# Two heads' blocks of 64 queries in one tile of 128 partitions, and 64 attention steps for 80

## The chip, the cores and the metric

The kernel runs on one core of a Trainium2 chip. The core's engines have a queue of instructions each and meet at semaphores: TensorE (PE in the profile; PEld is its loading of stationary operands), VectorE (DVE), ScalarE (ACT), GpSimd (POOL) and SyncE (SP), which here issues the DMAs. The metric is the device time of one execution in microseconds (us).

## What is computed

Causal attention over B=4 batches, H=8 heads, S=576 tokens and D=64, blended per head with a read of a linear memory, and behind it two gated MLPs over all 2304 tokens. In short:

```
a      = softmax(q k^T / 8, causal);  local = a v
q_p    = phi(q)                       # phi(x) = max(x, 0) + exp(min(x, 0))
mem    = (q_p M_prev) / (q_p . z_prev + 1e-6)
x      = g mem + (1 - g) local        # g = sigmoid(beta) of the head; heads side by side: 2304 x 512
x      = (sigmoid(x w_gate) * (x w_val)) w_out        # 512 -> 1536 -> 512
h      = x w_in;  out = (h * clip(h + 3, 0, 6) / 6) w_out2    # 512 -> 2048 -> 512
```

## The kernel before

The program has three phases. Phase A does the attention and, laid between its pieces, the gate and value products of the first MLP (the first half of its hidden features, six of twelve groups of 128, for the first 1872 tokens, in six chunks of 312). Phase B does the rest of the first MLP, phase C the second MLP.

Two heads are handled together, one in partitions 0 to 63 of the transposed queries and keys, the other in 64 to 127. The 576 query rows of a head are cut into blocks (`QB`): block 0 has 64 rows, blocks 1 to 4 have 128. Blocks 0, 1, 2 are the first range, 3 and 4 the second. A visit is one pair of heads and one range; there are 32 visits, and in each batch the four pairs' first ranges come before the four second ranges (`VISITS`). A block of a visit is a step: three steps in a visit of the first range, two in one of the second, 80 in all. A step does for its block and both heads:

- scores (`score_part`, L259): one matmul a head with 128 stationary query columns, into a PSUM tile of a pool of four which the MoE's products also use. For block 0 the stationary operand holds rows 64 to 127 too, which are not used later;
- one pass of DVE over each score tile, which adds the causal mask, scales and takes the row's extreme (L263), and one exponential a head on ACT with the row's sum (L280).

After the range's last step DVE makes the reciprocals of the sums with the gate's factor (L303, L304), and the rows are normalized (`normalize`), on ACT in steps 6 to 33 and for block 4, else on DVE (L309, L311). In the same rows, left of the attention weights, stand 64 columns of phi(q) over its norm (`prep_phi`, `memory_rows`; DVE, ACT and GpSimd), so that the memory read and the weighted sum of v are one product. Three steps later PE transposes the rows (`transpose_bank`, L322), up to four 128x128 pieces to a PSUM bank, ACT copies each bank to SBUF (L325), and the value products follow (`pv`, L348). Their result is stored to DRAM as `xd`, and a chunk of the MoE reads it back (`moe_x`, `xc<-xd`), splits it in a rounded part and a rest (L164, L165) and uses it two steps later at the earliest.

The order of PE's queue is that of the code in `phase_a`. A step is: scores, the transposes of two banks, a value product, then, if more is due, half of the step's share of MoE units, the rest of the scores and one more bank, then the other half of the share. A unit is three matmuls of 312 columns (L169 to L171). The share depends on the chunk (`FILL`). Where the next chunk is not there yet, no MoE unit is laid down. The order on DVE, ACT, GpSimd and SP is made by a scheduler. The first MLP's weights are loaded as pairs of 32-bit words and converted by DVE and ACT (`convert`, L134 to L143), one group every third step from step 6 on, nine groups.

Of the kernel before, what the change touches and what calls it, by code (L numbers as in the profile page):

```python
# [34 lines left out]

_T = [
    [(g, i, j) for g in range(2) for i, j in ((0, 0), (1, 0), (2, 0), (1, 1), (2, 1), (2, 2))],
    [(g, i, j) for g in range(2) for j in range(5) for i in (3, 4) if j <= i],
]
BANKS = [  # L40
    [_T[0][0:4], _T[0][4:8], _T[0][8:12]],
    [_T[1][4 * n : 4 * n + 4] for n in range(5)],
]
# [6 lines left out]
FILL = (4, 9, 6, 9, 6, 6)  # L50
# [10 lines left out]
PW = [384, 640]  # L61
# [4 lines left out]
class Kernel:  # L66
# [9 lines left out]
    def setup(self):  # L76
# [6 lines left out]
        self.bt_sb = cp.tile([128, H], F32, name="bt_sb")  # L83
# [4 lines left out]
    def attn_consts(self, pool):  # L88
# [14 lines left out]
        self.a1 = pool.tile([128, H], F32, name="a1")  # L103
        self.a2 = pool.tile([128, H], F32, name="a2")
# [77 lines left out]
    def load_visit(self, v):  # L182
# [6 lines left out]
        a = self.pa2.tile([128, 20 * D], F32, name="aux", tag="aux", bufs=3)  # L189
        qn = a[:, 0 : 10 * D].rearrange("p (e j d) -> p e j d", e=2, j=5)  # L190
        (t0, n), j0, j1 = RTOK[ranges[0]], RANGES[ranges[0]][0], RANGES[ranges[0]][-1] + 1
# [3 lines left out]
        if h == 0 and 0 in ranges:  # L195
            z = self.pa2.tile([128, H, D], F32, name="zz", tag="zz", bufs=1)
            nc.sync.dma_start(z, self.zz[b : b + 1].rearrange("o h d -> o (h d)").broadcast_to([128, H * D]))
            self.z = z
        nc.sync.dma_start(
            qn[:, :, j0:j1, :],  # L200
            src[:, 0 : 10 * D].rearrange("p (e j d) -> p e j d", e=2, j=5)[:, :, j0:j1, :],
        )
        v1 = 10 * D + j1 * 2 * D
        nc.sync.dma_start(a[:, 10 * D : v1], src[:, 10 * D : v1])
# [5 lines left out]
            "qn": qn,  # L210
            "v": a[:, 10 * D :].rearrange("p (j c) -> p j c", j=5),
        }

    def prep_phi(self, v):
# [5 lines left out]
        h0 = vs["pair"][1]  # L220
        blocks = [i for rg in vs["ranges"] for i in RANGES[rg]]
        nb = len(blocks)
        js = slice(blocks[0], blocks[-1] + 1)
        ph = self.pa2.tile([128, 2, nb, D], F32, name="ph", tag="ph")
        w = self.pa1.tile([128, 2, nb, D], F32, name="phw", tag="phw")
# [191 lines left out]
    def phase_a(self):  # L417
# [47 lines left out]
        while t < nt or tq or vq:  # L465
# [10 lines left out]
            if t < nt and i == RANGES[rg][1]:  # L476
                self.memory_rows(v, rg)
# [19 lines left out]
            if t >= 6 and t % 3 == 0:  # L497
                self.w_convert()
# [225 lines left out]
```

## Time and profile before

| | |
|---|---|
| median of 3 runs | 1108.28 us (1107.02 to 1108.61) |
| the profiled execution's own time | 1105.09 us |
| its span | 1103.3 us |
| PE busy | 1068.7 us, 97% |
| DVE busy | 625.0 us, 57% |
| ACT busy | 521.9 us, 47% |
| POOL busy | 58.5 us, 5% |
| mean granted PE clock | 0.991 of full speed |

The profiled execution is one run under the profiler; its span goes from the first to the last instruction that the profile shows, 1.8 us less than its time. PE's busy time counts a pipelined matmul until its modelled end, so 97% does not say that PE is at its peak. The shares are means over the whole span: phases B and C, from about 412 us on, are nearly PE alone, while DVE's and ACT's load lies in phase A. A granted clock of 1.00 is 2.4 GHz, 0.50 is 1.2 GHz.

### The profile page before, as it was taken

How to read it: one execution, taken by the hardware profiler on the slowest of the kernel's cores; microseconds unless marked ns; L12 is line 12 of the kernel's file. 1: busy time of each engine (PE TensorE's matmuls, PEld its weight loads, DVE VectorE, ACT ScalarE, POOL GpSimd, SP SyncE). 2: the span in 40 equal slices, each digit the busy share in tenths (PEclk: the TensorE clock that was granted, in tenths of full speed). 3: DMA queues.
4: the chain of work that ended last, by engine and by line, in shares of the span. 5: the costliest groups of instructions: out<-in, count | busy, mean ns of one | idle time of the engine just before them, and what ended most of it. 6: DMA issues, size and time to landing. Idle time of an engine off the chain costs nothing.

```text
span 1103.3 us, 16108 instructions
## 1 busy us (share of the span) xinstructions
PE 1068.7 (97%) x5984; PEld 921.0 (83%) x5984; DVE 625.0 (57%) x1526; ACT 521.9 (47%) x1161; POOL 58.5 (5%) x72
## 2 busy tenths in 40 slices
PE   6689999999999999999999999999999999999998
PEld 4357768887888789999888888999998999999897
DVE  7999975464546428988898348933232232322322
ACT  6899885557555645344443134433233232232322
POOL 2212111100110000000000000000000000000000
PEclk9889999999999999999999999999999999999999
DMA  6565532333233305334353224301001010010000
GB/s 218 165 212 164 192 111 84 109 89 102 83 102 94 91 15 206 115 108 163 131 188 112 70 89 154 110 1 58 1 1 58 1 58 1 21 37 1 29 1 29
DMA packets 58223, 98.54 MB, mean 89 GB/s; under 512 B 5665, under 2 KB 42529, under 8 KB 58145
## 3 DMA queue, kind: packets, MB, share of 16 engines
q1 hardware_dynamic: 58144, 97.51, 27.1%
q8 instruction: 47, 0.77, 0.3%
q14 instruction: 32, 0.25, 0.1%
HBM read 79.50 MB, written 17.99 MB: 88 GB/s over the span
## 4 chain that ended last, share of the span: by engine, by line
PE 84%; DVE 6%; DMA 4%; ACT 3%; issue 1%; SPq 0%; POOL 0%; ACTq 0%; DVEq 0%
PE g L171 12%; PE g L170 12%; PE g L169 11%; PE acc L647 6%; PE acc L648 6%; PE acc L649 6%; PE m L169 5%; PE m L171 4%; PE m L170 4%; PE pv L348 4%; PE t L322 3%; PE s L259 3%; PE acc L171 3%; PE acc L169 3%; PE acc L170 3%; DMA xc<-xd 2%
## 5 line engine op out<-in xcount | busy, mean ns | idle before, releaser
L170 PE MATMUL g<-xs,wslot 128*128 128x384 f32 (+2 forms) x672 | 235.3, 351 | 0.0
L171 PE MATMUL g<-xs,wslot 128*128 128x384 f32 (+2 forms) x672 | 235.3, 351 | 0.0
L169 PE MATMUL g<-xs,wslot 128*128 128x384 f32 (+2 forms) x672 | 230.7, 351 | 0.0
L636 DVE SCALAR_TENSOR_TENSOR th<-th,g 128x384 f32<-128x384 f32 x96 | 53.2, 554 | 219.8 <-ACT th L635 219.5
L635 ACT ACTIVATE th<-g,three 128x384 f32<-128x384 f32 x96 | 55.8, 581 | 219.6 <-PE g L171 218.7
L170 PEld LDWEIGHTS g<-xs,wslot 128*128 128x128 f32 x672 | 126.1, 188 | 9.2
L169 PEld LDWEIGHTS g<-xs,wslot 128*128 128x128 f32 x672 | 126.0, 188 | 8.7
L171 PEld LDWEIGHTS g<-xs,wslot 128*128 128x128 f32 x672 | 126.1, 188 | 6.8
L647 PE MATMUL acc<-wslot,hs 128*128 128x512 f32 x288 | 113.7, 395 | 0.0
L648 PE MATMUL acc<-wslot,hs 128*128 128x512 f32 x288 | 113.5, 394 | 0.0
L164 ACT CAST hs<-th 128x384 fp32r<-128x384 f32 (+2 forms) x132 | 69.9, 529 | 87.0 <-DVE th L636 49.6
L649 PE MATMUL acc<-wslot,hs 128*128 128x512 f32 x288 | 109.0, 393 | 0.0
L280 ACT ACTIVATE P<-P,m 128x64 f32<-128x64 f32 (+4 forms) x160 | 89.4, 561 | 35.2 <-DVE m L263 32.7
L165 DVE TENSOR_TENSOR hs<-th,hs 128x384 fp32r<-128x384 f32 (+2 forms) x132 | 76.1, 577 | 49.9 <-ACT hs L164 49.3
L169 PE MATMUL m<-xs,wslot 128*128 128x312 f32 x288 | 94.3, 327 | 0.0
L322 PEld LDWEIGHTS t<-ident,P 128*128 128x128 f32 x480 | 57.0, 147 | 38.6 <-issue 24.5
L322 PE MATMUL t<-ident,P 128*128 128x128 f32 x480 | 73.8, 291 | 15.3 <-issue 10.1
L170 PE MATMUL m<-xs,wslot 128*128 128x312 f32 x288 | 88.2, 306 | 0.0
L171 PE MATMUL m<-xs,wslot 128*128 128x312 f32 x288 | 87.9, 305 | 0.0
L259 PE MATMUL s<-qk 64*128 64x320 f32 (+4 forms) x384 | 78.8, 468 | 8.2 <-DMA qk<-in_qk 5.9
L263 DVE CUSTOM_DVE_ANT_0 P<-s,mask 128x320 f32<-128x320 f32 (+3 forms) x160 | 65.6, 429 | 17.3 <-PE s L259 16.8
L325 ACT COPY T<-t 128x512 f32<-128x512 f32 (+2 forms) x128 | 66.1, 541 | 9.8 <-PE t L322 9.7
(74 smaller groups left out, 1768.7 us busy)
## 6 DMA issues: line engine op xcount, KB each, us to landing
wst<-in_wm SPq DMA_DIRECT2D x68, 512.0 KB, 4.4
aux<-in_aux SPq DMA_DIRECT2D x32, 192.0 KB, 2.6
qk<-in_qk SPq DMA_DIRECT2D x32, 160.0 KB, 2.5
aux<-in_aux SPq DMA_DIRECT2D x16, 320.0 KB, 3.3
qk<-in_qk SPq DMA_DIRECT2D x16, 288.0 KB, 3.2
x<-x SPq DMA_DIRECT2D x6, 768.0 KB, 4.5
out<-xp SPq DMA_DIRECT2D x18, 256.0 KB, 2.0
xc<-xd SPq DMA_DIRECT2D x24, 156.0 KB, 2.2
```

The costliest lines, as they stand in the source:

```text
L164: (ehi.copy if ehi is self.nc.scalar else ehi.tensor_copy)(hi, src)
L165: elo.tensor_tensor(lo, src, hi.bitcast(F32), op=ALU.subtract)
L169: nc.tensor.matmul(out, w[0], x[0], start=first, stop=False)
L170: nc.tensor.matmul(out, w[0], x[1], start=False, stop=False)
L171: nc.tensor.matmul(out, w[1], x[0], start=False, stop=last)
L259: nc.tensor.matmul(ps[:, : e - a], qk[rows, 0, q0 : q0 + 128], qk[rows, 1, a:e], start=True, stop=True)
L280: self.nc.scalar.activation(x, x, AF.Exp, bias=vs["m", rg][:, g, n : n + 1], scale=-1.0, accum_out=vs["l", rg][:, g, n : n + 1],)
L322: nc.tensor.transpose(ps[:, c : c + 128], src, self.ident)
L325: nc.scalar.copy(pr["T", rg][:, o : o + c], ps[:, :c])
L647: nc.tensor.matmul(a, gs[:, 0, cc], w[:, 0, :], start=(f == 0), stop=False)
L648: nc.tensor.matmul(a, gs[:, 0, cc], w[:, 1, :], start=False, stop=False)
L649: nc.tensor.matmul(a, gs[:, 1, cc], w[:, 0, :], start=False, stop=(f == FF2 - 1))
```

## The change

Block 0 of the two heads, 64 query rows each, now shares one tile of 128 partitions: head 0's rows in partitions 0 to 63, head 1's in 64 to 127. A range's rows are a list of tiles (`ROWS`): in the first range the shared one and blocks 1 and 2 of both heads, five tiles for six; in the second range four, as before. The shared tile has no step of its own. Its scores are two matmuls with 64 stationary columns and 64 moving ones, written into columns 192 to 255 of the PSUM tile that holds the second head's scores of block 1 (L299 of the changed kernel), and a third DVE pass with a mask of its own (`mask0`) and a third exponential belong to that step. So a first range has two steps, `UNITS` (0, 1) and (2), and the attention 64 steps. What follows is changed to fit: per-row gate factors and z_prev come laid out by tile from the host, z_prev in three DMAs; phi is computed for five tiles; the first range has 11 transposes for 12; in the value products' output head 1 has its blocks in order and head 0 has block 0 behind blocks 1 and 2, so that the store is three DMAs. The numbers counted in steps are set anew: MoE units a step (`FILL`), the steps in which ACT normalizes, and the weight conversion, every second step from step 5 on.

```diff
+ROWS = [[None] + [(g, i) for g in range(2) for i in (1, 2)], [(g, i) for g in range(2) for i in (3, 4)]]
 _T = [
-    [(g, i, j) for g in range(2) for i, j in ((0, 0), (1, 0), (2, 0), (1, 1), (2, 1), (2, 2))],
+    [(1, 0), (2, 0), (0, 0), (3, 0), (4, 0), (1, 1), (2, 1), (3, 1), (4, 1), (2, 2), (4, 2)],
...
+UNITS = [[(0, 1), (2,)], [(3,), (4,)]]
...
-FILL = (4, 9, 6, 9, 6, 6)
+FILL = (5, 9, 8, 9, 8, 8)
...
+        self.mask0 = pool.tile([128, 64], F32, name="mask0")
+        for g in range(2):
+            rows = slice(64 * g, 64 * g + 64)
+            nc.gpsimd.tensor_copy(self.mask0[rows], self.mask[rows, 448 + 64 * g : 512 + 64 * g])
...
+            nc.sync.dma_start(flat(z[:, 0:H]), one(self.zz[b : b + 1, 0:H]).broadcast_to([128, H * D]))
+            for g in range(2):
+                h0 = H + H // 2 * g
+                nc.sync.dma_start(
+                    flat(z[64 * g : 64 * g + 64, H:]),
+                    one(self.zz[b : b + 1, h0 : h0 + H // 2]).broadcast_to([64, H // 2 * D]),
+                )
...
+        if rg == 0:
+            nc.gpsimd.tensor_tensor(w[:, 0], ph[:, 0], vs["z"][:, H + h0 // 2], op=ALU.mult)
+        r0 = nb - 4
+        z = vs["z"][:, h0 : h0 + 2, :].unsqueeze(2).to_broadcast([128, 2, 2, D])
+        heads = lambda a: a[:, r0:].rearrange("p (g n) d -> p g n d", g=2)
+        nc.gpsimd.tensor_tensor(heads(w), heads(ph), z, op=ALU.mult)
...
+    def row_max(self, v, rg, r, ps, a, e, mask):
+        m = self.visits[v]["m", rg][:, r : r + 1]
+        self.nc.vector.tensor_tensor_reduce(
+            out=self.row(v, rg, r, 64 + a, 64 + e),
+            in0=ps,
+            in1=mask,
...
             nc.tensor.matmul(ps[:, : e - a], qk[rows, 0, q0 : q0 + 128], qk[rows, 1, a:e], start=True, stop=True)
             tiles.append(ps)
+        if i == 1:
+            for g in range(2):
+                rows = slice(64 * g, 64 * g + 64)
+                nc.tensor.matmul(
+                    tiles[1][rows, e : e + 64], qk[rows, 0, 0:64], qk[rows, 1, 0:64], start=True, stop=True, skip_group_check=True
+                )
         for g, ps in enumerate(tiles):
+            self.row_max(v, rg, ROWS[rg].index((g, i)), ps[:, : e - a], a, e, self.mask[:, off + a : off + e])
+        if i == 1:
+            self.row_max(v, rg, 0, tiles[1][:, e : e + 64], 0, 64, self.mask0)
...
-        for g in range(2):
-            x = vs["P", rg][:, g, n, 64 : 128 + 128 * i]
+        for r in [ROWS[rg].index((g, i)) for g in range(2)] + [0] * (i == 1):
+            x = self.row(v, rg, r, 64, row_at(rg, r)[1])
...
             if rg == 0:
-                T = pr["T", rg][:, 704 * g : 704 * g + 704]
-                mine = [(0, 0, T[:, 0:320]), (1, 64, T[:, 320:576]), (2, 192, T[:, 576:704])]
+
+                o = 64 * g
+                mine = [(0, 0, 320 * g, 320), (1, o, 640 + 256 * g, 256), (2, o + 128, 1152 + 128 * g, 128)]
...
-        nc.sync.dma_start(self.xd[h // 2, :, b * S + t0 : b * S + t0 + nt], x[:, :nt])
+        dst = self.xd[h // 2, :, b * S + t0 : b * S + t0 + nt]
+        if rg == 0:
+            nc.sync.dma_start(dst[64:], x[64:, :nt])
+            nc.sync.dma_start(dst[:64, 64:], x[:64, : nt - 64])
+            nc.sync.dma_start(dst[:64, :64], x[:64, nt - 64 : nt])
+        else:
+            nc.sync.dma_start(dst, x[:, :nt])
...
-        steps = [(v, rg, i) for v, (p, ranges) in enumerate(VISITS) for rg in ranges for i in RANGES[rg]]
+        steps = [(v, rg, u[-1]) for v, (p, ranges) in enumerate(VISITS) for rg in ranges for u in UNITS[rg]]
...
-                    self.normalize(v, rg, 6 <= t < 34)
+                    self.normalize(v, rg, 5 <= t < 27)
...
-            if t >= 6 and t % 3 == 0:
+            if t >= 5 and t % 2:
                 self.w_convert()
```

On PE, in batch 0 before the MoE starts, one round of a first-range visit reads like this (s are scores, t transposes of an earlier visit, pv its value products). Before:

```order
L259 MATMUL s<-qk 128x192 x2
L259 MATMUL s<-qk 128x320 x2
L322 MATMUL t<-ident,P 128x128 x12
L259 MATMUL s<-qk 128x64 x2
L348 MATMUL pv<-T,aux 64x320 x2
L348 MATMUL pv<-T,aux 64x256 x2
L348 MATMUL pv<-T,aux 64x128 x2
```

And now:

```order
L294 MATMUL s<-qk 128x192 x2
L299 MATMUL s<-qk 64x64 x2
L352 MATMUL t<-ident,P 128x128 x11
L294 MATMUL s<-qk 128x320 x2
L376 MATMUL pv<-T,aux 64x320 x2
L376 MATMUL pv<-T,aux 64x256 x2
L376 MATMUL pv<-T,aux 64x128 x2
```

The scores of 64 columns have moved behind those of 192, with half the stationary columns; the transposes stand between the two steps of the visit, and the value products behind its second one.

On ACT the first instructions of the attention (P is the tile of weights, phw belongs to phi) were:

```order
L280 ACTIVATE P,l<-P,m 128x64 x2
L230 ACTIVATE phw<-phw 128x384
L280 ACTIVATE P,l<-P,m 128x192 x2
L280 ACTIVATE P,l<-P,m 128x320 x2
L230 ACTIVATE phw<-phw 128x384
```

And now:

```order
L312 ACTIVATE P,l<-P,m 128x192 x2
L312 ACTIVATE P,l<-P,m 128x64
L248 ACTIVATE phw<-phw 128x320
L312 ACTIVATE P,l<-P,m 128x320 x2
L312 ACTIVATE P,l<-P,m 128x192 x2
```

A visit has one exponential of 64 columns for two, and phi's is 320 wide for 384.

On SP, after the first visit's queries and keys (zz is z_prev; aux holds the rows for phi and M_prev with v), before:

```order
L197 DMA zz<-in_zz 128x512
L199 DMA aux<-in_aux 128x2x192
L204 DMA aux<-in_aux 128x384
L193 DMA qk<-in_qk 128x320
L194 DMA qk<-in_qk 128x320
```

And now:

```order
L213 DMA zz<-in_zz 128x512
L216 DMA zz<-in_zz 64x256 x2
L222 DMA aux<-in_aux 128x320
L224 DMA aux<-in_aux 128x384
L207 DMA qk<-in_qk 128x320
```

Two more DMAs stand ahead of the first aux loads, the first of which is smaller.

## Rows read from the trace of the kernel before

**Rows 1.** Stretches: length, busy PE, PEld, DVE, ACT, POOL, PEclk, DMA share, GB/s.

```profile
0.00:25.00 25.00, 16.75 (x74) 10.53 (x74) 17.79 (x66) 14.82 (x45) 7.07 (x13) 1.00 0.67 231
25.00:150.00 125.00, 106.44 (x664) 75.35 (x665) 119.78 (x315) 109.94 (x275) 22.86 (x23) 0.93 0.55 176
175.00:409.00 234.00, 232.48 (x1640) 192.25 (x1638) 115.20 (x432) 136.74 (x361) 25.56 (x32) 1.00 0.29 85
409.00:1103.00 694.00, 689.75 (x3450) 625.38 (x3449) 358.06 (x660) 240.78 (x436) 0.00 (x0) 1.00 0.20 69
```

**Rows 2.** Waits of PE, 175 to 409 us: total us, times, longest.

```profile
PE t L322 <- ACT T L325: 1.3, 3, 0.5
```

**Rows 3.** Order of time: start, us, engine, line, operation, count [idle before <-releaser].

```profile
152.98 0.45 ACT L164 CAST xs<-xc 128x312 fp32r<-128x312 f32 x1 [1.10 <-DMA xc<-xd]
...
153.97 0.44 PE L322 MATMUL t<-ident,P 128*128 128x128 f32 x2 [1.38 <-ACT T L325]
...
160.42 0.41 PE L169 MATMUL m<-xs,wslot 128*128 128x312 f32 x1
```

**Rows 4.** Groups by form: count | busy us, mean ns | idle before.

```profile
L280 ACT ACTIVATE P<-P,m 128x64 f32<-128x64 f32 x32 | 11.0, 344 | 7.2 <-DVE m L263 6.9
L231 DVE SCALAR_TENSOR_TENSOR ph<-aux,phw 128x384 f32<-128x384 f32 x16 | 10.0, 627 | 3.8 <-ACT phw L230 3.7
L234 DVE TENSOR_REDUCE nr<-phw 128x6 f32<-128x384 f32 x16 | 8.7, 546 | 2.9 <-POOL phw L233 2.8
L231 DVE SCALAR_TENSOR_TENSOR ph<-aux,phw 128x256 f32<-128x256 f32 x16 | 7.4, 461 | 2.5 <-ACT phw L230 2.3
L234 DVE TENSOR_REDUCE nr<-phw 128x4 f32<-128x256 f32 x16 | 6.6, 415 | 4.1 <-POOL phw L233 4.1
L263 DVE CUSTOM_DVE_ANT_0 P<-s,mask 128x64 f32<-128x64 f32 x32 | 6.2, 216 | 4.0 <-PE s L259 3.8
L311 DVE TENSOR_SCALAR P<-P,l 128x64 f32<-128x64 f32 x20 | 5.0, 250 | 0.3
L309 ACT ACTIVATE P<-P,l 128x64 f32<-128x64 f32 x12 | 4.1, 340 | 3.8 <-DVE l L304 3.8
```

**Rows 5.** Order of time at the start: an issue on SP, phi's first instruction.

```profile
2.11 0.43 SPq L197 DMA_DIRECT2D zz<-in_zz  x1
...
7.12 0.36 DVE L229 TENSOR_SCALAR phw<-aux 128x384 f32<-128x384 f32 x1 [1.88 <-DMA aux<-in_aux]
```

**Rows 6.** Order of time on PE in a first-range visit of batch 2.

```profile
220.00 0.60 PE L322 MATMUL t<-ident,P 128*128 128x128 f32 x4
220.35 0.39 PE L169 MATMUL m<-xs,wslot 128*128 128x312 f32 x1
...
221.44 0.31 PE L170 MATMUL m<-xs,wslot 128*128 128x312 f32 x1
221.59 0.30 PE L171 MATMUL m<-xs,wslot 128*128 128x312 f32 x1
221.82 0.44 PE L259 MATMUL s<-qk 64*128 64x64 f32 x4
222.19 1.41 PE L348 MATMUL pv<-T,aux 128*64 128x320 f32 x12
223.52 0.41 PE L169 MATMUL m<-xs,wslot 128*128 128x312 f32 x1
223.77 0.31 PE L170 MATMUL m<-xs,wslot 128*128 128x312 f32 x1
```

**Rows 7.** DMA issues by line: count, KB each, median us to landing.

```profile
xd<-xpr SPq DMA_DIRECT2D x16, 160.0 KB, 2.9
```

**Rows 8.** Waits of PE, 25 to 150 us.

```profile
PE t L322 <- issue: 10.1, 2, 5.3
...
PE s L259 <- DVE m L263: 1.4, 2, 0.8
```

**Rows 9.** Order of time on PE after an idle stretch.

```profile
34.35 3.15 PE L322 MATMUL t<-ident,P 128*128 128x128 f32 x12 [5.33 <-issue]
```

More of the change, by code (lines that the diff above doesn't have):

```diff
@@ L219, in prep_phi @@
         vs = self.visits[v]
[L220 to L225, printed above, removed]
-        nr = self.pa2.tile([128, 2, nb], F32, name="nr", tag="nr")
-        half = lambda a: a.rearrange("p e j d -> p e (j d)")
-        qn = vs["qn"][:, :, js, :]
@@ L229, in prep_phi @@
-        nc.vector.tensor_scalar_min(half(w), half(qn), 0.0)
-        nc.scalar.activation(half(w), half(w), AF.Exp)
-        nc.vector.scalar_tensor_tensor(half(ph), half(qn), 0.0, half(w), op0=ALU.max, op1=ALU.add)
-        z = vs["z"][:, h0 : h0 + 2, :].unsqueeze(2).to_broadcast([128, 2, nb, D])
-        nc.gpsimd.tensor_tensor(w, ph, z, op=ALU.mult)
+        h0, rg = vs["pair"][1], vs["ranges"][0]
+        nb = len(ROWS[rg])
+        ph = self.pa2.tile([128, 5, D], F32, name="ph", tag="ph")[:, :nb]
@@ L237, in prep_phi, with new_weights @@
+        nc.vector.scalar_tensor_tensor(nr, nr, 1e-6, self.a2[:, c0 : c0 + nb], op0=ALU.add, op1=ALU.mult)
         nc.vector.reciprocal(nr, nr)
-        vs["ph"], vs["nr"], vs["j0"] = ph, nr, blocks[0]
+        vs["ph"], vs["nr"] = ph, nr
+    def new_weights(self, v, rg):
+        vs, nb = self.visits[v], len(ROWS[rg])
+        vs["P", rg] = self.pa2.tile([128, 2304], F32, name="P", tag="P", bufs=3)
+        vs["l", rg] = self.pa2.tile([128, 5], F32, name="l", tag="l")[:, :nb]
+        vs["m", rg] = self.pa2.tile([128, 5], F32, name="m", tag="m")[:, :nb]
@@ new lines, in row @@
+    def row(self, v, rg, r, a, e):
+        return self.visits[v]["P", rg][:, row_at(rg, r)[0] + a : row_at(rg, r)[0] + e]
+    def row_max(self, v, rg, r, ps, a, e, mask):
[4 more added lines that the diff above has]
+            in1=mask,
+            scale=-0.125,
+            scalar=3.0e38 if a == 0 else m,
+            op0=ALU.add,
+            op1=ALU.min,
+            accum_out=m,
+        )
@@ L318, in transpose_bank @@
         ps = self.ps_t.tile([128, 512], F32, name="t", tag="t")
-        c = 0
-        for g, i, j in BANKS[rg][k]:
-            src = pr["P", rg][:, g, i - RANGES[rg][0], 128 * j : 128 * j + 128]
-            nc.tensor.transpose(ps[:, c : c + 128], src, self.ident)
-            c += QB[i][1]
-        o = sum(QB[i][1] for bk in BANKS[rg][:k] for g, i, j in bk)
-        nc.scalar.copy(pr["T", rg][:, o : o + c], ps[:, :c])
+        bank = BANKS[rg][k]
+        for n, (r, j) in enumerate(bank):
+            nc.tensor.transpose(ps[:, 128 * n : 128 * n + 128], self.row(v, rg, r, 128 * j, 128 * j + 128), self.ident)
+        c = 128 * len(bank)
+        nc.scalar.copy(pr["T", rg][:, 512 * k : 512 * k + c], ps[:, :c])
     def pv(self, v, rg):
@@ L699, in _arrays @@
         "aux": aux,
-        "zz": np.ascontiguousarray(i["z_prev"]),
-        "bt": bt,
+        "zz": np.ascontiguousarray(zz),
+        "bt": np.ascontiguousarray(bt.reshape(128, -1)),
         "wm1": bits(wm1),
```

162 lines of the change are left out of this document (78 added, 84 removed).

## The prediction

> **What bounds the kernel now.** I read the stretches of the span first [rows 1], then what TensorE (PE) waits for late in the attention [rows 2], then single places in order of time [rows 3], and then the forms of the instructions that go [rows 4]. The stretches fall into three parts. From 409 us to the end PE is busy nearly throughout at a granted clock of 1.00, and the change touches nothing there. From 175 to 409 us it is the same with attention in it: 232.48 of 234.00 us busy, and the only wait listed comes to 1.3 us in all [rows 2]. There a microsecond of PE work is a microsecond of the kernel. From 25 to 150 us PE has only 106.44 of 125 us, at a mean clock of 0.93, while VectorE (DVE) has 119.78 and ScalarE (ACT) 109.94: weight conversions, softmax and the first MoE chunk share these two, and this part ends when they are through. In the first 25 us DVE is busy for 17.79 us only.
>
> What ends the middle part is to be seen in order of time [rows 3]: while the MoE has run out of work, until chunk 1 can be had, ACT waits 1.10 us for a piece of the reloaded chunk, PE waits 1.38 us for a copy that stands behind it on ACT, and the MoE is under way again at 160.42 us. When that restart comes is decided by DVE and ACT; what follows it, by PE.
>
> **The early part (0 to 160 us).** Eight visits of the first range lie ahead of the restart, four of batch 0 and four of batch 1. Each gives up one set of instructions that are 64 wide. On DVE that is one maximum of 0.22 us, and the phi instructions get narrower, 320 elements for 384, half the way to the 256 that the trace has too: (627 - 461)/2 = 83 ns and (546 - 415)/2 = 66 ns, 0.15 us a visit [rows 4]. In the first two visits the normalization is DVE's too, 0.25 us each. DVE is relieved of 8 x (0.22 + 0.15) + 2 x 0.25 = 3.5 us. On ACT each visit loses an exponential of 0.34 us, and six of the eight a normalization of 0.34 us [rows 4]: 8 x 0.34 + 6 x 0.34 = 4.8 us. One instruction over both heads' halves costs what one over a half did, so it is the count that matters.
>
> Neither engine is full alone; each waits for the other in turn. If what they save is spent waiting for PE or a load, the gain is 0; if the two form one chain, it is the sum, 8.3 us. I take 4.5 us, near the ACT figure, since DVE and ACT together fill 230 of 250 us here and PE has room.
>
> Against that stands the start. z_prev takes three DMAs on SyncE's queue for one, ahead of the first visit's aux loads; an issue takes 0.43 us, and DVE already waits 1.88 us for that aux [rows 5]. Two more issues are up to 0.9 us where little covers them; but DVE now does wider maxima before it comes to that wait. I take 0.5 us (0 to 0.9). The two small GpSimd copies that build the second mask fall in the time of the first loads, so I cost them at nothing; without that cover they are two copies, once. Phi's product on GpSimd is split in a 64-wide and a 256-wide one, on an engine that is busy for 22.86 of 125 us [rows 1]: nothing, and if DVE's sum came to wait for it, one short instruction a visit.
>
> **The PE-bound part (160 to 409 us).** Eight more visits of the first range, in batches 2 and 3. Each had three steps and has two. A step with a third bank of transposes calls the MoE twice, so a visit had four MoE stretches and has three. To leave the MoE for a score takes 0.23 us from start to start (221.59 to 221.82), where two MoE matmuls are 0.15 apart (221.44 to 221.59): 0.08 more. To come back takes 0.25 (223.52 to 223.77), 0.10 more [rows 6]. One stretch less saves 0.18 us. Transposes are 11 for 12; four take 0.35 us (220.00 to 220.35), so 0.09 for one. The pair of 64-column scores took 0.37 us (221.82 to 222.19). In its place comes a pair over 64 columns again, with 64 stationary columns for 128, written beside the second head's scores of block 1. No row shows this shape. From below it costs nothing, if it runs beside its neighbours, a gain of 0.37; from above 0.37 and one more change of shape at 0.10, a loss of 0.10. I take 0.37, the nearest row, and no gain. A visit then saves 0.27 us (0.17 to 0.64), eight save 2.2 us (1.4 to 5.1).
>
> The Trainium skill, TensorEngine Tiling (Array Packing), Tiling Modes, says that a change of the tiling mode drains TensorE, which speaks against the new pair; the 0.08 and 0.10 us at a change [rows 6] agree with a price of that kind. By that rule the new pair brings one change and the dropped step takes two away, and the sum would be about 0.1 us a visit better, 0.8 us in all.
>
> The value products keep 320, 256 and 128 columns, and the copies of the transposes stay three, of 1408 columns in all. The first range's result is stored by three DMAs for one. Behind these on SyncE's queue stand the next visit's loads and the weights; two more issues of 0.43 us [rows 5] beside a landing of 2.9 us [rows 7] are hidden, except where a chunk waits for its last store. At the restart there are 7 us between the last split of the reloaded chunk on ACT (152.98) and the MoE (160.42) [rows 3]. I take nothing; if that cover were gone it would be 0.9 us at each of four places.
>
> **Sum.** The profiled execution took 1105.1 us: 1105.1 - 4.5 + 0.5 - 2.2 = 1098.9. It lies 3.2 us below the median of the runs shown, 1108.3, so the forecast is 1102.1 us, 0.56% less. This case's own range, with 1 to 8 us from the early part, is 1097 to 1106.
>
> **Rivals.** First, the early gain is lost to another wait: DVE and ACT are freed, but the restart still comes at the pace of loads, or of the chain of the first chunk through memory. For it: 10.1 us of PE's waits there have no releaser that the profile shows [rows 8]. Against it: DVE's 119.78 of 125 us [rows 1]. Then 1108.3 - 2.2 + 0.5 = 1106.6.
>
> Second, more than the sum. After an idle stretch PE runs at the lower of its two clocks, 1.2 GHz: the twelve transposes at 34.35 us took 3.15 us, 0.26 each, three times what they take late [rows 6, 9]. The mean of 0.93 over 25 to 150 us is 8.8 us of full-rate PE time lost. Where visits close up some of this comes back, say 1.5 us, and with the early part at its upper bound and 3.5 us from PE: 1108.3 - 8.3 - 3.5 - 1.5 = 1095.
>
> Third, slower: score tiles in PSUM. Block 1's second tile now holds block 0 too, and DVE reads it once more before it is free; the four tiles of that pool also take the MoE's sums. The further pass is 0.22 us [rows 4], and up to a microsecond more with what DVE's queue has between. If PE waits 0.8 us for a tile in each of 16 visits, that is 12.8 us, and 1102.1 + 12.8 = 1114.9; it decides from 6.2/16 = 0.39 us a visit. Against it: scores waited 1.4 us for DVE's maxima from 25 to 150 us [rows 8], not at all after 175 us [rows 2], and a visit now takes four score tiles for six.
>
> Fourth, slower: the stores. One of the three pieces has rows of 64 elements, 256 bytes. If its landing doubled, by 2.9 us [rows 7], and nothing hid that where the first chunk and the three next batches wait: 1102.1 + 4 x 2.9 = 1113.7. Against it are the 7 us [rows 3]. The Trainium skill, DMA: Bandwidth & Descriptors, Specifications, wants at least 512 bytes in a transfer for full rate and tells of a read-modify-write below that; no row here shows a store with such rows by itself.
>
> That the change doesn't do what it says is ruled out by the order: 11 transposes for 12, and two score steps for three, stand in it.
>
> **Chances.** Forecast 0.55, early gain lost 0.17, more 0.15, PSUM 0.09, stores 0.04. About 0.2%, 2.2 us, is what a measurement of this kernel can tell from no change. Faster: 0.55, half of the first rival and the second, 0.78. Slower: the third and fourth and little of the first, 0.12; the rest, 0.10, is the same. The range goes from the second rival's time to a little past the first's, 1095 to 1108; the two slower rivals and the tails are left out.
>
> **What would show it.** The restart of the MoE comes at 154 to 159 us and not at 160.42. DVE runs 176 maxima for 192, PE 464 transposes for 480. From the start of the new pair to what follows it 0.3 to 0.45 us. The attention ends 7 to 12 us earlier than 409, since by the order 47 groups of three MoE matmuls come behind its last value product in place of 39, each 0.43 us, on top of the gain. Waits of PE for DVE's maxima above 3 us after 160 us would speak for the third rival, waits of ACT for the reloaded chunk above 3 us at a batch's end for the fourth. The forecast is wrong if the restart is not at least 2 us earlier.

## The result and the profile after

The changed kernel took 1093.96 us (median of 4, 1093.89 to 1094.87) against 1107.65 us for the one before (median of 4, 1104.21 to 1108.61): a ratio of 0.9884, 95% interval 0.9861 to 0.9906, a gain of 13.7 us. The forecast was 1102.1 us with a range of 1095 to 1108. The direction was right; the gain is twice as large, and the time lies 1 us outside the range. The profiled execution took 1093.92 us, its span 1092.1 us.

The stretches of the kernel after, which answer to [rows 1] (length, then busy PE, PEld, DVE, ACT, POOL, granted clock, DMA share, GB/s; the third goes to the end of the attention, now 394 us):

```profile
25.00:150.00 125.00, 106.95 (x673) 75.73 (x671) 118.35 (x314) 109.89 (x263) 25.61 (x30) 0.92 0.57 180
175.00:394.00 219.00, 218.13 (x1567) 181.37 (x1566) 104.56 (x392) 128.04 (x331) 22.98 (x37) 1.00 0.30 88
```

The early stretch looks as it did: DVE and ACT as full, the clock as low (0.92). Fuller engines or a better clock are not where the gain is; the same stretch of time now holds more of the work. That is seen at the restart, in order of time as in [rows 3] (start, us, engine, line, operation):

```profile
150.01 0.45 ACT L178 CAST xs<-xc 128x312 fp32r<-128x312 f32 x1 [0.25 <-DMA xc<-xd]
...
151.09 1.06 PE L352 MATMUL t<-ident,P 128*128 128x128 f32 x8
...
154.18 0.41 PE L183 MATMUL m<-xs,wslot 128*128 128x312 f32 x1
```

ACT waits 0.25 us for the last reloaded piece, not 1.10, PE not at all for the copy behind it, and the MoE is under way again at 154.18 us instead of 160.42.

What PE waits for from 160 to 394 us, which answers to [rows 2], and from 25 to 150 us, which answers to [rows 8] (total us, times, longest):

```profile
PE m L184 <- DVE ha L179: 0.9, 1, 0.9
```

```profile
PE pv L376 <- ACT T L354: 7.8, 7, 2.4
PE t L352 <- POOL P L327: 5.1, 1, 5.1
PE s L294 <- DVE m L274: 4.5, 3, 3.7
PE pv L376 <- ACT xpr L385: 0.3, 1, 0.3
```

The new pair of scores late in the attention, which answers to [rows 6], and the last value products:

```profile
162.99 0.31 PE L185 MATMUL m<-xs,wslot 128*128 128x312 f32 x1
163.22 0.60 PE L294 MATMUL s<-qk 64*128 64x192 f32 x4
163.75 0.33 PE L299 MATMUL s<-qk 64*64 64x64 f32 x4
164.01 0.77 PE L352 MATMUL t<-ident,P 128*128 128x128 f32 x5
...
393.73 1.08 PE L376 MATMUL pv<-T,aux 128*64 128x256 f32 x8
```

From the start of the pair to what follows it are 0.26 us, where the old one took 0.37. And the forms that were to go [rows 4], with phi's new width (count | busy us, mean ns | idle before):

```profile
L249 DVE SCALAR_TENSOR_TENSOR ph<-aux,phw 128x320 f32<-128x320 f32 x16 | 7.8, 487 | 3.9 <-ACT phw L248 3.7
L256 DVE TENSOR_REDUCE nr<-phw 128x5 f32<-128x320 f32 x16 | 7.7, 479 | 3.8 <-POOL phw L255 3.8
L312 ACT ACTIVATE P<-P,m 128x64 f32<-128x64 f32 x16 | 5.6, 347 | 0.0
L274 DVE CUSTOM_DVE_ANT_0 P<-s,mask 128x64 f32<-128x64 f32 x16 | 3.5, 217 | 0.0
L340 ACT ACTIVATE P<-P,l 128x64 f32<-128x64 f32 x6 | 2.1, 352 | 0.0
```

16 for 32 maxima, at 217 ns for 216; 16 for 32 exponentials, at 347 for 344: one instruction over both heads costs what one over a half did, as forecast. Phi's two, 320 wide, take 487 and 479 ns, where half the way gave 544 and 481.

Where the time went, between the two profiled spans (1103.3 and 1092.1, 11.2 us): the restart is 6.24 us earlier; from the restart to the end it is 942.9 before and 937.9 after, 5.0 less. The other 2.5 us of the 13.7 come from the choice of the execution: the profiled one of before is 2.6 us quicker than its median, that of after lies on its own. A second profile of the kernel before (e0 below, an execution of 1110.13 us) has the restart at 163.8 us and 944.5 us behind it, 3.4 and 1.6 later than the first. So against a usual run of before the gain is larger on both sides of the restart, and a mark of before is known to no better than these differences.

### The profile page after: what moved, and what is told of

Same layout as the page of the kernel before. It is cut to its first block, busy times and chain, and to the rows that moved or that the text cites. A ratio compares the mean times of both kernels' runs of the same rounds, so it can differ in the third digit from the quotient of the medians.

```text
span 1092.1 us, 16040 instructions
## 1 busy us (share of the span) xinstructions
PE 1060.6 (97%) x5968; PEld 916.2 (84%) x5968; DVE 613.0 (56%) x1484; ACT 514.3 (47%) x1123; POOL 58.9 (5%) x90
## 4 chain that ended last, share of the span: by engine, by line
PE 88%; DVE 6%; ACT 3%; DMA 1%; issue 1%; SPq 0%; ACTq 0%; DVEq 0%
PE g L185 12%; PE g L183 12%; PE g L184 12%; PE acc L690 6%; PE acc L691 6%; PE acc L692 6%; PE m L183 5%; PE m L184 5%; PE m L185 5%; PE t L352 4%; PE s L294 4%; PE pv L376 4%; PE acc L183 3%; PE acc L185 3%; PE acc L184 3%; ACT P L312 1%
## 5 line engine op out<-in xcount | busy, mean ns | idle before, releaser
L312 ACT ACTIVATE P<-P,m 128x192 f32<-128x192 f32 (+4 forms) x144 | 84.0, 587 | 37.7 <-DVE m L274 37.5
L294 PE MATMUL s<-qk 64*128 64x320 f32 (+3 forms) x320 | 71.4, 505 | 12.0 <-DMA qk<-in_qk 7.2
L352 PE MATMUL t<-ident,P 128*128 128x128 f32 x464 | 69.5, 289 | 5.5 <-POOL P L327 5.1
L376 PE MATMUL pv<-T,aux 128*64 128x256 f32 (+2 forms) x512 | 63.5, 374 | 8.6 <-ACT T L354 8.3
L274 DVE CUSTOM_DVE_ANT_0 P<-s,mask 128x320 f32<-128x320 f32 (+3 forms) x144 | 62.5, 452 | 16.5 <-PE s L294 16.0
```

The costliest lines, as they stand in the source:

```text
L294: nc.tensor.matmul(ps[:, : e - a], qk[rows, 0, q0 : q0 + 128], qk[rows, 1, a:e], start=True, stop=True)
L312: self.nc.scalar.activation(x, x, AF.Exp, bias=vs["m", rg][:, r : r + 1], scale=-1.0, accum_out=vs["l", rg][:, r : r + 1])
L352: nc.tensor.transpose(ps[:, 128 * n : 128 * n + 128], self.row(v, rg, r, 128 * j, 128 * j + 128), self.ident)
L376: nc.tensor.matmul(ps[rows, o : o + w], pr["v"][:, j, rows], T[:, c : c + w], start=(n == 0), stop=(n == last), skip_group_check=True,)
```

## The experiments

The queues of DVE, ACT, GpSimd and SP are ordered by a scheduler, so every edit moves more than it says. Each run is therefore read by the same marks: the end of the ninth and last weight conversion of the first MLP on DVE; the restart; the span behind it; ACT's waits for reloaded pieces (`xs<-xc`) from 100 us to the restart; PE's waits there for a converted weight (`wslot`). All marks are from one profile a run. Ratios are to the kernel before on the same chip.

| run | median us | ratio [95%] | 9th conv. | restart | restart to end | ACT: xc | PE: weight |
|---|---|---|---|---|---|---|---|
| before | 1107.65 | 1 | 128.2 | 160.4 | 942.9 | 1.4 | 1.9 |
| e0 before again | 1105.67 | 0.9991 [0.9978, 1.0005] | 130.0 | 163.8 | 944.5 | 3.4 | 1.9 |
| n3 before, nudged | 1106.82 | 0.9993 [0.9982, 1.0003] | 127.3 | 162.7 | 942.4 | 1.6 | 0 |
| z2 before, cadence | 1107.01 | 0.9986 [0.9977, 0.9995] | 130.0 | 163.2 | 943.3 | 1.8 | 1.5 |
| y2 before, splits on GpSimd | 1105.26 | 0.9975 [0.9965, 0.9984] | 122.1 | 164.0 | 938.9 | 0 | 0 |
| x2 before, hold | 1114.26 | 1.0056 [1.0043, 1.0069] | 130.2 | 169.4 | 943.1 | 6.9 | 1.9 |
| e2 merged steps only | 1108.3 | 1.0009 [0.9996, 1.0022] | 131.6 | 165.2 | 941.6 | 1.3 | 3.0 |
| x5 e2, hold | 1110.23 | 1.0027 [1.0015, 1.0039] | 131.5 | 167.8 | 939.8 | 1.8 | 3.0 |
| e1 shared tile only | 1104.91 | 0.9976 [0.9966, 0.9987] | 125.5 | 164.3 | 938.9 | 3.2 | 3.6 |
| z1 e1, cadence | 1099.79 | 0.9923 [0.9912, 0.9935] | 125.5 | 161.0 | 939.0 | 0.6 | 3.7 |
| x3 e1, hold | 1101.43 | 0.9940 [0.9925, 0.9956] | 123.5 | 159.3 | 940.0 | 1.1 | 4.1 |
| **after** | 1093.96 | 0.9884 [0.9861, 0.9906] | 121.9 | 154.2 | 937.9 | 1.0 | 0 |
| x1 after, hold | 1092.31 | 0.9859 [0.9845, 0.9873] | 120.0 | 151.4 | 938.8 | 0.3 | 0 |
| n2 after, nudged | 1097.34 | 0.9908 [0.9893, 0.9924] | 123.2 | 156.6 | 938.9 | 0.4 | 5.8 |
| e5 after, extra transpose | 1098.14 | 0.9908 [0.9895, 0.9921] | 123.5 | 157.3 | 939.1 | 1.1 | 6.1 |
| e6 after, extra ACT | 1099.74 | 0.9919 [0.9906, 0.9932] | 124.9 | 158.3 | 938.2 | 0.6 | 7.8 |
| e9 after, extra DVE | 1097.05 | 0.9899 [0.9887, 0.9912] | 125.7 | 157.6 | 937.6 | 0.7 | 6.6 |
| e8 after, own PSUM tile | 1099.21 | 0.9925 [0.9911, 0.9938] | 121.4 | 159.4 | 938.6 | 3.0 | 0 |
| e7 after, one store | 1101.89 | 0.9936 [0.9918, 0.9954] | 123.2 | 162.4 | 938.6 | 4.2 | 0 |
| y1 after, hold, splits on GpSimd | 1096.94 | 0.9891 [0.9878, 0.9904] | 125.2 | 155.5 | 939.7 | 0 | 3.3 |

**The two halves of the change.** e0 is the kernel before once more; e1 shares the tile and keeps 80 steps with the old pacing; e2 keeps the tiles apart and makes two steps of a visit, with the new pacing.

```diff
 e1: change, with
-UNITS = [[(0, 1), (2,)], [(3,), (4,)]]   -FILL = (5, 9, 8, 9, 8, 8)
+UNITS = [[(0,), (1,), (2,)], [(3,), (4,)]]   +FILL = (4, 9, 6, 9, 6, 6)
 e2: before, block 0's two score pieces at columns 192:256 of block 1's two tiles
+tiles[g][:, 192:256], qk[rows, 0, 0:128], qk[rows, 1, 0:64]
```

> The kernel before, once more, for a second profile and more times. Its four times so far run from 1104.2 to 1108.6 us, those of the change only from 1093.9 to 1094.9. Theory A (clock): the spread comes from low-clock intervals in the stretch 25 to 170 us that fall on more or less urgent PE work; then this profile differs from the first in that stretch and nowhere behind it by more than 0.5 us. Theory B (loads): the spread lies in DMA landing times, seen as other waits for DMA in the first 160 us. Expected time 1104 to 1109 us either way.

> The shared tile alone: block 0 of both heads in one tile, but with a step of its own, 80 steps, and the MoE shares, conversions and ACT steps of the kernel before. Theory W (less work): the gain is the removed instructions (16 transposes, 16 maxima, 32 fewer 64-wide ACT instructions), so this run has most of it: 9 to 12 us below before, 1096 to 1099 us. Theory S (steps): the gain is that a visit has fewer and longer steps, so this run has only what PE saves by 11 transposes and the cheaper score pair, 8 x 0.2 us, and up to 3 us early: 2 to 5 us below before, 1103 to 1106 us.

> Two steps a visit without the shared tile: block 0 of each head keeps its own 128 rows (half unused), its scores stand in columns 192 to 255 of that head's tile of block 1, six tiles, 12 transposes, four maxima and four exponentials in the first step; 64 steps with the MoE shares, conversions and ACT steps of the change. Theory W: 1 to 3 us below before, 1105 to 1107 us. Theory S: 8 to 11 us below before, 1097 to 1100 us. If the two effects simply add, e1 and e2 together give the 13.7 us of the change.

e0: the kernel before repeats to 0.1% in the median, but its runs scatter from 1103.65 to 1110.13 us; after's from 1093.9 to 1094.9. Its second profile differs by 1.6 us behind the restart, which theory A excludes; theory B's sign is there (ACT waits 3.4 us for reloaded pieces, not 1.4), but what the scatter comes from was not tried. e1 gains 2.4 parts in a thousand, as theory S had it for a kernel without the merged steps; but e2, which has them, gains nothing, where S gave 8 to 11 us. So neither theory holds. The parts do not add up to the whole. Behind the restart they nearly do: e1 is 4.0 us shorter there, e2 1.3 (less than the 1.6 between two profiles of one kernel), the change 5.0. Up to the ninth conversion e1 is 2.7 us ahead of before, the change 6.3, e2 behind. What e1 was ahead it lost before the restart. On ACT in e1, in order of time:

```profile
140.59 0.45 ACT L178 CAST xs<-xc 128x312 fp32r<-128x312 f32 x1 [2.86 <-DMA xc<-xd]
158.63 0.45 ACT L178 CAST xs<-xc 128x312 fp32r<-128x312 f32 x1 [0.38 <-DMA xc<-xd]
```

and PE in e1, 100 to 160 us (total us, times, longest):

```profile
PE m L185 <- DVE wslot L157: 3.6, 1, 3.6
PE pv L377 <- ACT T L355: 2.0, 1, 2.0
PE t L353 <- ACT T L355: 1.8, 1, 1.8
```

PE waits 3.6 us for a weight. ACT stands 2.86 us for one reloaded piece, up to 140.59 us, and from there to the copy of transposes at 148.17, for which PE waits 2.0, it has no gap; exponentials and normalizations lie between. That the 2.86 us reach PE by way of that queue is argued from this and not shown.

**Less for DVE and ACT before the restart.** The "hold" opens the second phase's pool ahead of its staging buffers, so that its conversions do not come between the last visits.

```diff
-        self.stage, self.wide = self.pool(ctx, "wstage2", 2), 1
         self.bx = self.pool(ctx, "bx", 1)
+        self.stage, self.wide = self.pool(ctx, "wstage2", 2), 1
```

> The change with phase B's conversions held back. Theory Q: the restart (154.2 us) comes 3 to 6 us earlier and the kernel is at 1088 to 1091 us, and its distance to x2 is about the sum of x3's and x5's, 8 to 12 us. Theory I: 1092 to 1094 us, and the distance to x2 stays 12 us or more. If the phase behind the attention then lacks converted weights, PE waits for wslot after 400 us would show it.

> The kernel before, with one swap: the pool for the x chunks of phase B is opened ahead of phase B's weight staging, so that the staging lies in memory that the attention still uses. In every run so far four half groups of phase B's weights are converted between the 12th and 15th visit (before: 133 to 154 us), in the middle of the stretch that DVE and ACT bound; with the swap they come behind the attention. They are 4 x 2.7 us on DVE and 4 x 0.7 on ACT. Theory Q (queue): the part of the change's gain that neither the shared tile nor the merged step gave alone comes from where these conversions fall in the queues; taken out, the MoE restarts (160.4 us before) at about 152 and the kernel is 5 to 9 us faster, 1098 to 1102 us. Theory I (interaction of the two parts): the conversions fill gaps, and this is within 3 us of before.

> The shared tile with a step of its own (80 steps), and phase B's conversions held back as in x2. Theory Q: the shared tile's early 4 us, seen at the 12th visit's normalization, now reach the restart, and with the 4 us of the PE-bound part this is 7 to 9 us below x2. Theory I: 2 to 4 us below x2, as without the hold.

> Two steps a visit, no shared tile, phase B's conversions held back. Theory Q: the merged step gives its late 1.3 us and nothing early: 0 to 3 us below x2. Theory I: within 2 us of x2 too; this run tells how the effects add: with x3 and x1, whether the change is the sum of its parts.

One edit, four answers: 1.7 us faster in the change, 3.5 faster in e1, 2 slower in e2, 6.6 slower in before (in e2 and in the change the intervals of the ratios overlap). Theory Q, that the held conversions stood in the way, forecast 5 to 9 us less for before and is refuted there; x1's time is that of theory I. x3 lies 12.8 us below x2, where the two theories gave 7 to 9 and 2 to 4. Less work ahead of the restart does not mean an earlier restart. In before with the hold ACT's waits for reloaded pieces rose from 1.4 to 6.9 us:

```profile
128.75 0.45 ACT L164 CAST xs<-xc 128x312 fp32r<-128x312 f32 x1 [1.10 <-DMA xc<-xd]
141.62 0.45 ACT L164 CAST xs<-xc 128x312 fp32r<-128x312 f32 x1 [3.59 <-DMA xc<-xd]
160.02 0.45 ACT L164 CAST xs<-xc 128x312 fp32r<-128x312 f32 x1 [2.24 <-DMA xc<-xd]
```

The change with the hold, 1092.31 us (1091.68 to 1093.56), is the fastest of all; against before that is clear, against the change it is not.

**Where the conversions stand, and who splits the reloaded pieces.**

```diff
 z1 (e1), z2 (before): at the places of the change
-            if t >= 6 and t % 3 == 0:
+            if t >= 7 and t % 5 in (2, 4):
 y2 (before), y1 (change with hold):
-            self.split(t[:, 0], t[:, 1], x, self.nc.scalar, self.nc.vector)
+            self.split(t[:, 0], t[:, 1], x, self.nc.gpsimd, self.nc.gpsimd)
```

> Shared tile with a step of its own (80 steps), and the weights converted at the same places of the visits as in the change (behind the scores of blocks 2 and 4) in place of every third step. Theory C: in the shared-tile kernel with its own step, what was gained before the twelfth visit (4 us) was lost again because PE waited 3.6 us for a converted weight; conversions earlier take that wait away, the restart comes at 159 to 161 us instead of 164.3 and the time is about 3.5 us less, 1101 to 1102 us. Rival, theory M: the conversions' places are worth nothing by themselves, and what the change gains over the shared tile alone comes from the shorter visits: 1104 to 1106 us, restart at 163 to 165 us.

> The kernel before with the weights converted at the same places of the visits as in the change (behind the scores of blocks 2 and 4) in place of every third step; nothing else. Theory C: PE's one wait for a converted weight in the first chunk (1.9 us) goes, 1105 to 1106 us, and the scatter of the kernel before (7 us) gets smaller. Rival, theory M: within 1 us of the kernel before, or 1 to 2 us slower, since DVE and ACT get more to do in the same time.

> The kernel before with both instructions that split a reloaded piece of a chunk (the copy on ScalarE and the subtraction on VectorE) moved to GpSimd, which is busy for 22.86 of 125 us there. Theory R: ScalarE's queue stands behind its waits for the reloaded pieces (1.4 to 3.4 us in two profiles), and copies of transposes behind it, for which PE waits; off ScalarE the restart comes 1.5 to 3 us earlier, at 157.5 to 159 us, and the time is 1104.5 to 1106 us with less scatter. Rival, theory G: GpSimd takes about twice as long for a piece (0.68 to 0.98 us where DVE takes 0.47), the chunk is ready later by 1 to 2 us, 1107.5 to 1110 us.

> The change, with the second phase's conversions held until the attention is through (as in the run before, 1092.31 us) and both instructions that split a reloaded piece on GpSimd. Theory R: ScalarE waits only 0.3 us for reloaded pieces there, so there is little to win: 1091 to 1092.5 us at most 1 us better. Rival, theory G: the splits on GpSimd make each of the chunks ready later, 1 us at each of four places behind it: 1093 to 1096 us.

z1 came out at the time that theory C gives and better, yet not by its mechanism: PE still waits 3.7 us for the weight, and the ninth conversion ends at 125.5 as in e1. What went is ACT's wait for a reloaded piece (3.2 to 0.6 us), and the restart came 3.4 us earlier. In before the same edit is worth 1.5 us. y2 bears theory R out by its time (3.2 us less than before on the same chip) and not by its mark: the restart is not earlier, but the part behind it is 4.0 us shorter. y1 is 4.6 us slower than x1, somewhat more than theory G gave: from 100 us to the restart GpSimd itself waits 13.4 us for pieces, and PE 3.3 us for a weight, which it does not in x1.

**Adding back what the change took, and taking away its stores.** e8 gives the shared tile's scores a PSUM tile of their own; e6, e9 and e5 add instructions in each first-range visit; e7 stores in one piece.

```diff
 e8
-                    tiles[1][rows, e : e + 64], qk[rows, 0, 0:64], qk[rows, 1, 0:64], ...
+                    ps0[rows, 0:64], qk[rows, 0, 0:64], qk[rows, 1, 0:64], ...
 e6, twice in a first-range visit
+                nc.scalar.activation(d, self.mask[:, 0:64], AF.Exp)
 e9, twice in a first-range visit
+                nc.vector.tensor_scalar_mul(d, self.mask0, self.ident[:, 0:1])
 e5, once in a first-range visit
+            nc.tensor.transpose(ps[:, 384:512], self.row(v, rg, 4, 256, 384), self.ident)
 e7
-            nc.sync.dma_start(dst[64:], x[64:, :nt])   (and the two others)
+            nc.sync.dma_start(dst, x[:, :nt])
```

> The change, with block 0's scores in a PSUM tile of their own instead of columns 192 to 255 of the second head's tile. If holding that tile for a third pass costs PE waits (third rival of the prediction, which did not come), this is faster by up to 3 us; if sharing the tile saves a place in the pool of four, it is slower by 1 to 5 us, since the step takes three tiles at once. Expected: 1094 to 1097 us, same to slightly slower.

> The change, and two 64-wide exponentials more on ScalarE in each of the 16 first-range visits (into a scratch tile, 0.34 us each), which is about what the change took from ScalarE. Theory A: ScalarE's count is what the early part is paid by; the 12th visit's normalization goes from 122.6 back to 126 to 127 us, the restart to 157 to 159 us, and the time is 1097 to 1100 us. Rival, theory K: ScalarE waits for others often enough to hide it, and the gain is of the shorter visits themselves: normalization at most 1 us later, 1094 to 1095.5 us.

> The change, and two 64-wide multiplications more on VectorE in each of the 16 first-range visits (into a scratch tile), behind the maximum of the shared tile; about what the change took from VectorE (a maximum of 0.22 us and 0.15 us of the phi instructions a visit). Theory D: VectorE is as much on the early path as ScalarE, the 12th visit's normalization 2 to 4 us later, 1096 to 1099 us. Rival, theory K: hidden, 1093.5 to 1095 us.

> The change, and a twelfth transpose in each of the 16 first-range visits (a piece once more, into columns of the bank that nothing reads), so that PE runs as many transposes as before. By the prediction's price, 0.09 us a transpose, the PE-bound part is 8 x 0.09 = 0.7 us longer and the early part the same: 1094.5 to 1095 us. Rival: a transpose costs nothing beside its neighbours, 1094.0 us; or it stands on the chain from the transposes to the value products in the early part at the low clock, 0.26 us each, 8 x 0.26 = 2.1 us more: 1096 to 1097 us.

> The change with one store in place of three for the first range's result (head 0's columns then land with the first 64 at the end, so that what the MoE gets is in another order; the work is the same). By the prediction the three stores cost nothing: within 0.5 us of the change, 1093.5 to 1094.5 us. Rival, the fourth of the prediction: the extra issues or the 64-wide rows lie on the path of the reloaded chunks; without them it is 1 to 4 us faster, 1090 to 1093 us.

All five are 3 to 8 us slower than the change, e7 with less work by 7.9 us; e5, e7 and e8 lie outside every range given for them. Behind the restart none differs from it by more than 1.2 us. e8 and e7 stand for pieces on ACT, here e8 (in e7 the store of 160 KB lands in 3.3 us, where the three pieces take 2.4 to 2.9; how much of the 7.9 us is that and how much the order was not separated):

```profile
133.29 0.45 ACT L178 CAST xs<-xc 128x312 fp32r<-128x312 f32 x1 [3.02 <-DMA xc<-xd]
```

e5, e6 and e9 let PE stand for a weight, 6.1 to 7.8 us, here e6:

```profile
PE m L183 <- ACT wslot L154: 4.5, 1, 4.5
PE m L185 <- DVE wslot L157: 3.3, 1, 3.3
```

e6 and e9 land in the times that theories A and D give, but not by their mark: the twelfth visit's sums, at 122.6 us in the change, were to come later and come at 115.1 and 117.6. And e5 with one transpose is nearly as slow. That is too alike for five different causes.

**The order alone.** The nudge is one addition of zero to a few row sums in the third visit, 0.13 us on DVE once in the kernel.

```diff
         l, nb = pr["l", rg], len(ROWS[rg])
+        if v == 2:
+            self.nc.vector.tensor_scalar_add(l, l, 0.0)
```

> The change, and one addition of zero to the few row sums of the third visit on VectorE, an instruction of some 0.06 us, once in the whole kernel. By the order of the rows this nudge moves 197 of VectorE's 1486 instructions, 77 of ScalarE's 981 and 20 of SyncE's 388 against each other; PE's order is untouched. Theory O (order): part of the 13.7 us is the order that the scheduler happened to give the three queues; another order without any more work costs 2 to 6 us, 1096 to 1100 us, with waits of 3 us or more of PE for a converted weight, or of ScalarE for a reloaded piece, before the restart. Rival, theory K: the runs with work added back were slower for the work; the nudge changes nothing, 1093.5 to 1095 us.

> The kernel before with the same nudge in the third visit, which moves 169 of VectorE's 1528 instructions, 74 of ScalarE's 1003 and 10 of SyncE's 348. Theory O: the time moves by 2 to 6 us in either direction, since the order before is one of many too: 1102 to 1106 or 1110 to 1114 us. Rival, theory K: within 1 us of the kernel before, 1107 to 1109 us.

The nudge costs the change 3.4 us (1097.34, all four runs within 0.6 us of each other; before took 1107.63 us on that chip, so the chips do not explain it). Before it leaves where it was, against theory O, which gave 2 to 6 us there. So in the change the order alone does what e5 and e9 did. How, is to be seen on DVE, first of after (start, us, line, operation):

```profile
120.68 1.21 DVE L157 TENSOR_TENSOR wslot<-wst,wslot 128x1024 fp32r<-128x1024 f32 x1
121.81 0.47 DVE L438 SCALAR_TENSOR_TENSOR th<-th,m 128x312 f32<-128x312 f32 x1
122.20 0.48 DVE L249 SCALAR_TENSOR_TENSOR ph<-aux,phw 128x320 f32<-128x320 f32 x1
122.60 0.15 DVE L335 SCALAR_TENSOR_TENSOR l<-l,a 128x5 f32<-128x5 f32 x1
```

then of the nudged kernel:

```profile
117.32 0.43 DVE L337 SCALAR_TENSOR_TENSOR l<-l,a 128x5 f32<-128x5 f32 x1
...
122.00 1.21 DVE L157 TENSOR_TENSOR wslot<-wst,wslot 128x1024 fp32r<-128x1024 f32 x1
```

After's queue finishes the ninth weight (121.9) and then turns to the twelfth visit's sums (122.60). The nudged one has these sums 5.3 us earlier and the weight 1.3 us later; its MoE, also ahead, then stands for that weight, here on PE:

```profile
117.19 0.31 PE L184 MATMUL m<-ha,wslot 128*128 128x312 f32 x1
123.27 0.63 PE L185 MATMUL m<-ha,wslot 128*128 128x312 f32 x1 [5.77 <-DVE wslot L157]
123.70 0.46 PE L183 MATMUL m<-ha,wslot 128*128 128x312 f32 x1
123.96 0.46 PE L184 MATMUL m<-ha,wslot 128*128 128x312 f32 x1
```

and pays again: the matmuls behind the idle stretch start 0.26 us apart, not 0.145. The stretches of the nudged kernel (columns as above, the granted clock third from the end):

```profile
117.00:123.00 6.00, 0.50 (x4) 0.24 (x2) 6.00 (x14) 5.07 (x14) 0.72 (x2) 0.93 0.10 27
123.00:127.00 4.00, 3.73 (x13) 2.55 (x15) 1.52 (x7) 0.57 (x2) 2.04 (x3) 0.50 0.65 228
127.00:131.00 4.00, 4.00 (x23) 2.31 (x22) 3.35 (x9) 1.27 (x3) 0.00 (x0) 0.75 0.96 352
```

and of after:

```profile
117.00:123.00 6.00, 5.32 (x34) 3.54 (x31) 6.00 (x14) 5.18 (x17) 0.97 (x2) 1.00 0.63 153
123.00:127.00 4.00, 4.00 (x31) 3.38 (x31) 2.53 (x11) 3.67 (x10) 1.49 (x3) 1.00 0.83 261
```

At 0.50 (1.2 GHz) for 4 us and a mean of 0.75 between the two levels for 4 more, 4 x 0.5 + 4 x 0.25 = 3 us of full-rate PE time are gone.

Over all the runs: the restart comes 30.3 to 36.3 us behind the ninth conversion where ACT waits less than 2 us for reloaded pieces, and 38.0 to 39.2 where it waits 3 us or more (e1, e8, e7, x2). Two do not fit: e0 (3.4 us, but 33.8) and y2 (41.9, where GpSimd does the waiting, as it does in y1 with 30.3). The two marks go together in most runs; that the one sets the other was not tried.

## Why the prediction missed, step by step

**Early part, 4.0 us forecast (4.5 less 0.5), 6.2 measured at the restart.** That DVE and ACT are full up to there, and that their instructions go at the prices of [rows 4], held. The first failed step is the 4.5 us, the relief of the two as a number for the restart. It took the restart as paid by busy time alone; it is also set by the order in which the queues hold the ninth weight, the visits and the reloaded pieces. With the nudge the restart is at 156.63, 3.8 us earlier than before and near the forecast, and 2.4 us behind the change; but that is one other order of many, and against the second profile of before it is 7.2 earlier. The order is luck, of the change as of the nudged kernel. How much ACT's or DVE's relief is worth by itself stays open: e6 and e9, which were to tell it, end 2.4 us above and 0.3 us below the nudged kernel, less than what an order moves.

**PE-bound part, 2.2 us forecast, 5.0 measured behind the restart (4.0 with the nudge).** The second failed step: the term held what instructions cost, and the waits behind the restart were taken as the 1.3 us of the view [rows 2] and put at nothing. Counted from start to start between the restart and the last value product, 248.6 us became 239.6; 24 MoE matmuls at 0.1435 us, 3.4 us, now stand behind that point, so 5.6 us are gained (0.6 of it comes back behind).

About 2.9 us of these are instructions. Fewer MoE stretches give 1.5 (1.4 forecast; the switches from the MoE to scores fell by 9, from 50 to 41, where 8 were forecast). Fewer transposes give 0.5 (0.7 forecast). The pairs of 64 columns give 8 x (0.37 - 0.26) = 0.9, where the prediction took nothing: the shape that no row showed lies between its bounds of 0 and 0.47.

The rest is waits. In two visits of before the set of value products took 2.15 us from its start to the next MoE matmul, where 1.33 is usual [rows 6], since the last copy of transposes stood on ACT behind two splits of reloaded pieces. Here is one of them; the other starts at 360.48:

```profile
249.01 0.80 ACT L164 CAST xs<-xc 128x312 fp32r<-128x312 f32 x2
249.52 2.22 PE L348 MATMUL pv<-T,aux 128*64 128x320 f32 x12
249.70 0.58 ACT L325 COPY T<-t 128x512 f32<-128x512 f32 x1
251.67 0.41 PE L169 MATMUL m<-ha,wslot 128*128 128x312 f32 x1
```

These are 1.6 us. Twice a transpose started 0.75 us behind its neighbour, where 0.11 is usual, 1.3 us; one set of 256-wide scores cost 0.7. In after no set of value products takes more than 1.34 and no transpose starts so late; it has one wait of its own, 1.0 us by the starts (0.9 in the view, for `ha`). Together that is 2.6 us. The view of waits shows less than the starts do, since it counts PE as busy up to a matmul's modelled end. "There a microsecond of PE work is a microsecond of the kernel" was nearly right; that PE's waits there were 1.3 us in all was not.

Sharing is one way to lose these waits and not the only one: all twelve kernels that share the tile lie at 937.6 to 940.0 us behind the restart, and of the eight that do not, six at 941.6 to 944.5. The other two are y2 (938.9), where the splits are off ACT, and x5 (939.8), with merged steps and the hold; in both the slow value products and late transposes are gone.

**The base.** 3.2 us between the profiled execution and the median were carried over to the changed kernel. Before scatters over 7 us, after over 1, and after's profiled execution lies on its median. So the miss is 8.1 us: 3.2 from the base and 5.0 between the 1098.9 forecast for a profiled execution and the 1093.9 measured. With the nudged kernel as the measure, 3.4 of the 5.0 are the order and 1.6 the rest; that division hangs on one other order.

**The start and GpSimd** cost nothing visible: the first MoE matmul comes at 64.4 us, 71.0 before. PE's transposes wait 5.1 us for GpSimd's rows in the early stretch, which the view of before does not name; but there they waited 10.1 us for something that it does not show [rows 8], so no loss is shown.

**The rivals.** The first (gain lost) is refuted by the restart. The second gave nearly the time (1095), with more from the early part (8.3) and less from PE (3.5) than came. Its third term, the clock, gave nothing from 25 to 150 us (0.93 to 0.92); from there to the restart it was 0.83 in before (150 to 160 us) and 1.00 in after. (The 0.26 us a transpose at 34.35 us that it read as the lower clock is more than that: the granted clock from 34 to 38 us was 0.50, a factor of two, and the transposes took three times their late time.) The third (PSUM) did not come: after 160 us PE waits for no maximum; early it waits 4.5 us where it was 1.4, and a tile of its own (e8) made nothing better. The fourth (stores): ACT waits 1.0 us for reloaded pieces before the restart, and behind it 5.0 us in four waits up to 394 us, the longest 2.1; in before these were 5.9 in four, so the new stores left no mark. How the new stores land in the kernel after, which answers to [rows 7] (count, KB each, median us to landing):

```profile
xd<-xpr SPq DMA_DIRECT2D x16, 80.0 KB, 2.9
xd<-xpr SPq DMA_DIRECT2D x16, 64.0 KB, 2.8
xd<-xpr SPq DMA_DIRECT2D x16, 16.0 KB, 2.4
```

The piece with 256-byte rows lands in 2.4 us, sooner than the whole did. The rule of the Trainium skill, DMA: Bandwidth & Descriptors, Specifications, that less than 512 bytes a transfer is not served at full rate, costs no time here that the rows show.

**The marks.** 464 transposes and 16 fewer maxima: as said. The pair in 0.3 to 0.45 us: 0.26, shorter. The Trainium skill, TensorEngine Tiling (Array Packing), Tiling Modes, had a change of mode drain TensorE; from the MoE to the score it is 0.23 us (162.99 to 163.22) as before, and the new pair, one mode more, brings no price of its own that shows. The attention ends 15.3 us earlier (409.01 to 393.73), not 7 to 12, in line with the larger gain.

## What to carry to other kernels

Where a scheduler orders the queues and two of them are full, a forecast made of instruction prices carries an error of the order itself: here 3.4 us for one instruction of 0.13 us in one kernel, nothing for the same in another, and 8 us for an edit that takes work away. Before a change is credited or blamed, or an edit of a few us is judged by one build, run it with a nudge that changes the order and no work. And ahead of a restart look for what stands in an in-order queue behind a wait on memory, and for the last converted weight, before adding up busy time. Where PE looks busy, compare like sets of matmuls from start to start: a set that takes 2.15 us where its like takes 1.33 holds a wait that the view of waits leaves out in part.

## What had not been expected of the hardware

A wait of PE can cost more than its length: in the nudged kernel PE was busy at the full 2.4 GHz up to 117 us, idle for 5.77, and then at 1.2 GHz: 3 us of full-rate time on top of the wait. Two 64-column matmuls with 64 stationary columns in the two halves of the rows take 0.26 us a pair, with 128 stationary columns 0.37.
